# Attention with an MLP mixer on one core: GpSimd's queue in program order, K in quarters, an earlier LN2, and other slots for sums and norm

## The chip, the cores and the metric

The kernel runs on one core of a Trainium2 chip. The metric is the device time of one execution in microseconds (us). The core has five engines that work side by side and wait for each other by semaphores: TensorE (PE, matrix products), VectorE (DVE, elementwise work), ScalarE (ACT, exp, tanh and the like), GpSimd (POOL) and SyncE (SP). DMA transfers are issued from the queues of SP, POOL or ACT.

## What is computed

With x of 2048 tokens by 512 features, K and V caches of 32 heads by 2048 keys by 128, the reference is, cut to what matters:

```
xn = layernorm(x)
q  = (xn @ wq) in 32 heads of 128
p  = softmax(q @ K^T / sqrt(128))          per head, 2048 x 2048
s  = concat(p @ V) @ wo
h  = gelu(layernorm(xn) @ w1)              four quarters of the features,
hs = concat(shifted quarters of h) @ w2    shifted by +1, -1, +2, -2 tokens
x1 = xn + hs
h2 = gelu(layernorm(x1) @ w3) @ w4         w3: 512 x 1792
out = x + s * silu(x1 + h2)
```

Inputs and output are bf16.

## The kernel before

**Units and slots.** The attention is cut into 128 units, each one head and one block of 512 queries (L113). Four heads form a group; a group goes through its four query blocks, and in each through its four heads. A unit has eight slots (SPU = 8, L54). The loop at L507 runs over all slots n; u, p = divmod(n, 8) are the unit and the slot in it. In each slot `s_slot` (L158) issues two score matmuls into one of two score buffers (psS) and the exp on ACT, and `pv_slot` (L187) issues two PV matmuls, five slots behind the scores (LAG = 5, L55). So the first PV of unit u is issued in slot 5 of unit u. Its sum over all keys is built in one PSUM bank, `ps_o`, from a pool of two (L95).

**What else a unit does.** The q projection of the next unit, `q_mm` (L145), in slots 0 and 1, and its copy to bf16, `q_copy` (L153), on DVE in slot 2. DVE adds up the exps of the unit: `add_first` in slot 4, `add_next` in slot 6, and `add_last` (L181) in slot 0 of the next unit, which is a last addition of 2048 columns and two folds (1024 and 512 columns). In slot 3 `sums` (L197) reduces over partitions with four small matmuls (ps_sum), takes the reciprocal on DVE (rc, L204) and sends it to DRAM (dr); in slot 4 `bcast` (L208) reads it back to all partitions (rb). In slot 2 of the unit after that, `norm` (L213) multiplies ps_o by rb into oT, and so frees the ps_o bank: norm(u-2) runs in unit u. After the four heads of a group, the output projection `wo_mm` (L223) of four token tiles takes slots 4 and 5 of the four following units, and `wo_post` (L240) adds it to the float32 sum s_acc in slot 6. The q projection, the sums and the output projection share one PSUM bank (tag xa of psX).

**The MLP** is cut into 136 chunks (L463 to L478), spread evenly over the half units (slots 2 and 3, or 6 and 7; W0 and W1 at L479): 16 of w1 (m1), 16 of the shifted mixer w2 (m2), then for each of four token blocks 14 of w3 (m3) and 12 of w4 (m4). `at(n, fn)` puts follow-up work into later slots: a GELU pair (L281) is a square and a tanh on ACT and two DVE operations, 3 and 7 slots after its matmuls. `ln2` (L378) loads four tiles of x1, normalises them on DVE and transposes them by DMA into xn2T. For the first token block it is called when the mixer's last chunk is done (hook "ph2", L561), together with the opening of the pool that takes the mixer's place (ph2), w4 and three w3 loads; the chunks wait for four half units there.

**Order of the queues.** `pin` (keep_in_program_order, L61) keeps the instructions of an engine in the order of the program. It is used for PE, DVE, ACT and SP work. What GpSimd issues (loads of V, Wq, Wo, the LN tiles, w1 to w4, the stores of xn, x1 and g, and the two operations of `rsqrt`, L108) is not pinned: the framework's scheduler orders it. K comes by transposing DMA on SP in four pieces of 512 keys (`load_k`, L123); in the last query block of a group, head hh of the next group is loaded in unit hh of the block, two pieces in slot 5 and two in slot 7 (L511 to L520).

**The start.** Four x tiles are loaded on SP and ACT and their LN statistics taken, then the loads of head 0, the normalised tiles (xnT by DMA transposes), the loads of heads 1 to 3, the mixer's weights and four Wo tiles. Tiles 4 to 15 are loaded (on GpSimd), measured and normalised in the first slots (L501).

Of the kernel before, what the change touches and what calls it, by code (L numbers as in the profile page):

```python
# [17 lines left out]
def kernel(  # L18
# [71 lines left out]
    gtp = ent(pool("gt", 2))  # L90
    tokp = ent(pool("tok", 3))
    drp = ent(pool("drp", 4, bass.MemoryType.DRAM))
    dsp = ent(pool("dsp", 1, bass.MemoryType.DRAM))
# [14 lines left out]
    def rsqrt(out, var):  # L108
        ve = smp.tile([P, 1], FP32, name="ve")
        nc.gpsimd.tensor_scalar(out=ve[:], in0=var, scalar1=EPS, scalar2=None, op0=ALU.add)  # L110
        nc.gpsimd.tensor_tensor(out=out, in0=ve[:], in1=nhalf[:], op=ALU.pow)

# [19 lines left out]
    def load_v(h):  # L132
        vBs[h] = vp.tile([P, KC, Dh], BF16, name="vb")
        nc.gpsimd.dma_start(  # L134
            out=vBs[h][:], in_=A_v_cache[0, h].rearrange("(kc p) d -> p kc d", p=P))

    def load_w(h):
        wqs[h] = wqp.tile([P, DC, Dh], BF16, name="wq_h")
        nc.gpsimd.dma_start(out=wqs[h][:], in_=wq_v[:, :, h * Dh:(h + 1) * Dh])  # L139

    def load_wo(h):
        wos[h] = wop.tile([P, D], BF16, name="wo_h")
        nc.gpsimd.dma_start(out=wos[h][:], in_=A_wo[h * Dh:(h + 1) * Dh, :])

# [35 lines left out]

    def add_last(u):  # L181
        add_next(u, 3)
        a = st[u]["acc"]
        pin(nc.vector.tensor_tensor(out=a[:, 0:2, :], in0=a[:, 0:2, :], in1=a[:, 2:4, :], op=ALU.add))  # L184
        pin(nc.vector.tensor_tensor(out=a[:, 0, :], in0=a[:, 0, :], in1=a[:, 1, :], op=ALU.add))  # L185
# [47 lines left out]
    def fin_load(t):  # L233
        xl = finp.tile([P, D], BF16, name="xl")
        nc.gpsimd.dma_start(out=xl[:], in_=xsrc[t])
        gl = finp.tile([P, D], BF16, name="gl")
        nc.gpsimd.dma_start(out=gl[:], in_=g_d[t][:])
        fin[t] = (xl, gl)
# [18 lines left out]

    def ln1_stats(t, eng):
        xin = tokp.tile([P, D], BF16, tag="xin", bufs=4, name="xin")
        eng.dma_start(out=xin[:], in_=xsrc[t])  # L260
        bn = smp.tile([P, nc.vector.BN_STATS_DIM], FP32, name="bn")
        mv = smp.tile([P, nc.vector.BN_AGGR_DIM], FP32, name="mv")
        rs = smp.tile([P, 1], FP32, name="rs")
        pin(nc.vector.bn_stats(out=bn[:], in_=xin[:]))
        pin(nc.vector.bn_aggr(out=mv[:], in_=bn[:]))
        rsqrt(rs[:], mv[:, 1:2])
        ln[t] = (xin, mv, rs)

    def ln1_apply(t):
        xin, mv, rs = ln.pop(t)  # L270
        xn = tokp.tile([P, D], BF16, tag="xn", bufs=4, name="xn")
        pin(nc.vector.tensor_scalar(
            out=xn[:], in0=xin[:], scalar1=mv[:, 0:1], scalar2=rs[:],
            op0=ALU.subtract, op1=ALU.mult))
        pin(nc.sync.dma_start_transpose(out=xnT[:, :, t * P:(t + 1) * P], in_=xn[:]))
        nc.gpsimd.dma_start(out=xn_d[t][:], in_=xn[:])

# [49 lines left out]
    def ph1_load():  # L327
        nc.gpsimd.dma_start(out=w1_sb[:], in_=B_w1.rearrange("(dc p) j -> p dc j", p=P))
        nc.gpsimd.dma_start(out=w2_sb[:], in_=B_w2.rearrange("(jc p) c -> p jc c", p=P))
# [14 lines left out]
    def m2_chunk(t):  # L344
        def run(i, n):
            if i == 0:
                mlp["ps"] = psX.tile([P, 512], FP32, tag="xm", name="ps_m")
                mlp["xr"] = tokp.tile([P, D], BF16, tag="xr", bufs=3, name="xr")
                nc.gpsimd.dma_start(out=mlp["xr"][:], in_=xn_d[t][:])
            for jc in (2 * i, 2 * i + 1):  # L350
                c0 = BASE_J[jc] + t * P - SHIFT[jc]
                mm(mlp["ps"][:], hT[:, jc, c0:c0 + P], w2_sb[:, jc, :], jc == 0, jc == DC - 1)
            if i == 1:
                ps, xr = mlp["ps"], mlp["xr"]

                def x1():
                    pin(nc.vector.scalar_tensor_tensor(
                        out=xr[:], in0=ps[:], scalar=0.5, in1=xr[:], op0=ALU.mult, op1=ALU.add))
                    nc.gpsimd.dma_start(out=x1_d[t][:], in_=xr[:])

                def stats():
                    bn = smp.tile([P, nc.vector.BN_STATS_DIM], FP32, name="bn")
                    pin(nc.vector.bn_stats(out=bn[:], in_=xr[:]))
                    pin(nc.vector.bn_aggr(out=mv2[:, t, :], in_=bn[:]))
                    rsqrt(rstd2[:, t:t + 1], mv2[:, t, 1:2])

                at(n + 1, x1)
                at(n + 2, stats)
        return run

    def ph2_open():
# [3 lines left out]
        nc.gpsimd.dma_start(out=w4_sb[:], in_=B_w4.rearrange("(fc p) c -> p fc c", p=P))  # L375
        mlp.update(ph2=ph2, w4=w4_sb, h2={})

    def ln2(c, n):  # L378
        def start():
            mlp["xn2T"] = mlp["ph2"].tile([P, DC, 512], BF16, name="xn2T")  # L380
            xs = []
            for ts in range(4):
                xr = tokp.tile([P, D], BF16, tag="x1", bufs=4, name="x1r")
                nc.gpsimd.dma_start(out=xr[:], in_=x1_d[c * 4 + ts][:])
                xs.append(xr)
            mlp["xs"] = xs
# [33 lines left out]
    def w3_prefetch():  # L420
        if w3_order:
            c, fc = w3_order.popleft()
            w = mlp["ph2"].tile([P, DC, 2 * P], BF16, tag="w3", bufs=3, name="w3_sb")
            nc.gpsimd.dma_start(out=w[:], in_=w3_v[:, :, fc * P:(fc + 2) * P])  # L424
            mlp["w3next"][(c, fc)] = w
# [3 lines left out]
    def m4_chunk(t, part):  # L429
# [3 lines left out]
        def run(i, n):  # L433
            if part == 0 and i == 0:
                mlp["ps"] = psX.tile([P, 512], FP32, tag="xm", name="ps_m")
                mlp["xr"] = tokp.tile([P, D], BF16, tag="xr", bufs=3, name="xr")
                nc.gpsimd.dma_start(out=mlp["xr"][:], in_=x1_d[t][:])
            h = (len(fcs) + 1) // 2
# [3 lines left out]
            if part == 2 and i == 1:  # L442
# [10 lines left out]
                def silu():  # L453
                    pin(nc.vector.scalar_tensor_tensor(
                        out=xr[:], in0=th[:], scalar=1.0, in1=xr[:], op0=ALU.add, op1=ALU.mult))
                    nc.gpsimd.dma_start(out=g_d[t][:], in_=xr[:])

# [6 lines left out]
    for tt in range(QT):  # L464
        for jc in range(DC):
            chunks.append(m1_chunk(tt, jc))
    for t in range(NT):
        chunks.append(m2_chunk(t))
    hooks = {len(chunks): "ph2"}
    for c in range(QT):  # L470
# [12 lines left out]

    ln1_engs = [nc.sync, nc.scalar, nc.sync, nc.scalar]
    for t in range(4):
        ln1_stats(t, ln1_engs[t])
    load_w(0)
    load_k(0, range(KSPLIT))
    load_v(0)
    for t in range(4):  # L490
        ln1_apply(t)
    for h in range(1, HG):
        load_w(h)
        load_k(h, range(KSPLIT))
        load_v(h)
    ph1_load()
    for h in range(HG):
        load_wo(h)
    q_mm(0, range(DC))
    q_copy(0)  # L500
    for k, t in enumerate(range(4, NT)):  # L501
        n0 = 1 + 4 * k
        at(n0, lambda t=t: ln1_stats(t, nc.gpsimd))
        at(n0 + 4, lambda t=t: ln1_apply(t))

    wo_todo = deque()
    for n in range(NS + 3 * SPU):  # L507
        u, p = divmod(n, SPU)
        if u < NU:
            g, qt, hh = units[u]  # L510
            if g + 1 < NG and qt == QT - 1:  # L511
                h = (g + 1) * HG + hh
                if p == 5:
                    load_k(h, (0, 1))
                elif p == 6:
                    load_v(h)
                    load_w(h)
                elif p == 7:
                    load_k(h, (2, 3))
                    load_wo(h)  # L520
            s_slot(u, p)
# [5 lines left out]
        if p == 0 and 1 <= u <= NU:  # L527
            add_last(u - 1)
        if p == 2 and u + 1 < NU:
            q_copy(u + 1)  # L530
        if p == 2 and 2 <= u <= NU + 1:
            norm(u - 2)
            if units[u - 2][2] == HG - 1:
                gg, qq = units[u - 2][:2]
                wo_todo.extend((gg, 4 * qq + ts) for ts in range(4))
                if gg == NG - 1:
                    fin_load(4 * qq)
        if p == 3 and 1 <= u <= NU:
            sums(u - 1)
        if p == 4 and 1 <= u <= NU:  # L540
            bcast(u - 1)
        if p in (4, 5) and wo_todo:
            wo_mm(*wo_todo[0], (0, 1) if p == 4 else (2, 3))
        if p == 6 and wo_todo:
            gg, t = wo_todo.popleft()
            wo_post(gg, t)
            if gg == NG - 1 and t % 4 < 3:
                fin_load(t + 1)
        if p == 4 and u < NU:
            add_first(u)  # L550
# [63 lines left out]
```

## Time and profile before

| what | value |
|---|---|
| median of 3 runs (lowest, highest) | 1346.35 us (1344.34, 1347.98) |
| profiled execution: time, span | 1346.22 us, 1344.4 us |
| granted TensorE clock, mean | 0.985 |
| busy: PE, DVE, ACT, POOL | 95%, 76%, 83%, 16% |
| score matmuls (128x512) | 2048, mean 381 ns as recorded |
| exp on ACT (128x1024) | 1024, mean 1029 ns |
| addition on DVE (128x2048) | 1220 ns |
| norm on DVE (128x512) | 681 ns median |
| rb to landing, K piece to landing | 4.2 us, 4.8 us median |

The span runs from the first to the last instruction on the engines; the time of an execution is a little more. Matmuls are pipelined: one of 512 columns is recorded at 0.38 us, but a pair follows the pair before after 0.43 us. A wait is put down to the instruction whose end released it.

### The profile page before, as it was taken

What the parts mean: (1) busy time and instruction counts of PE and PEld (TensorE: products, weight loads), DVE (VectorE), ACT (ScalarE), POOL (GpSimd) and SP (SyncE); (2) the same over time, 40 slices, a digit from 0 to 9 for tenths busy, and PEclk for the clock granted to TensorE, in tenths of its full rate; (3) what the DMA queues carried; (4) which work ended last, traced back from release to release, by engine and by line L of the source; (5) the groups of instructions that cost most, each with busy time, mean ns of one, the idle gap of its engine ahead of it and who ended that gap; (6) DMA issues with size and microseconds to landing.
All of it is one profiled execution on the core that took longest, in us unless ns stands there. A gap on an engine that the chain in (4) does not pass through costs nothing.

```text
span 1344.4 us, 17137 instructions
## 1 busy us (share of the span) xinstructions
PE 1275.2 (95%) x6208; PEld 576.4 (43%) x6208; DVE 1024.1 (76%) x1402; ACT 1112.8 (83%) x1185; POOL 212.4 (16%) x343
## 2 busy tenths in 40 slices
PE   2899999999599999999999999999999999999996
PEld 1344444444244444444444444444444444444442
DVE  1898788887377886778877767888767788777886
ACT  2799988787399987889998888999878999888882
POOL 6620122323101012010111001110010100000111
PEclk9999999999799999999999999999999999999997
DMA  9830383326722239222473215522273222812223
GB/s 213 182 87 25 71 135 71 76 59 144 154 56 59 45 67 158 63 52 46 91 131 75 52 36 124 100 61 42 56 137 68 64 47 48 125 34 52 81 66 90
DMA packets 144260, 112.29 MB, mean 84 GB/s; under 512 B 112112, under 2 KB 114672, under 8 KB 144176
## 3 DMA queue, kind: packets, MB, share of 16 engines
q1 hardware_dynamic: 126496, 57.19, 24.3%
q0 software_dynamic: 17392, 53.76, 15.9%
q8 instruction: 48, 0.79, 0.3%
q14 instruction: 36, 0.29, 0.1%
q10 hardware_dynamic: 288, 0.26, 0.1%
HBM read 81.53 MB, written 8.65 MB: 67 GB/s over the span
## 4 chain that ended last, share of the span: by engine, by line
PE 74%; DVE 9%; DMA 8%; ACT 5%; issue 3%; POOL 1%; SPq 0%; DVEq 0%; POOLq 0%
PE ps_s L106 27%; PE ps_o L106 25%; PE ps_wo L106 8%; PE ps_m L106 8%; PE ps_q L106 6%; ACT pT L168 4%; DMA rb<-dr 3%; DVE acc L179 3%; DMA dr<-rc 2%; PE ps_sum L106 1%; DVE acc L184 1%; DVE qT L155 1%; DMA xin<-in_A_x_dram 1%; ACT sq L286 1%; DMA xn2T<-x1r 1%
## 5 line engine op out<-in xcount | busy, mean ns | idle before, releaser
L168 ACT ACTIVATE pT<-ps_s 128x1024 bf16<-128x1024 f32 x1024 | 1015.7, 1029 | 205.0 <-PE ps_s L106 200.4
L106 PE MATMUL ps_s<-qT,kT 128*128 128x512 bf16 x2048 | 612.1, 381 | 5.5 <-DVE qT L155 2.4
L106 PE MATMUL ps_o<-pT,vb 128*128 128x512 bf16 x2048 | 610.7, 380 | 0.0
L179 DVE TENSOR_TENSOR acc<-acc,pT 128x2048 bf16<-128x2048 bf16 x256 | 312.4, 1220 | 84.9 <-ACT pT L168 80.1
L106 PEld LDWEIGHTS <-vb 128*128 128x128 bf16 x2048 | 200.2, 98 | 243.6 <-issue 3.0
L106 PEld LDWEIGHTS <-kT 128*128 128x128 bf16 x2048 | 196.7, 98 | 245.3 <-issue 28.3
L174 DVE TENSOR_TENSOR acc<-pT 128x2048 bf16<-128x2048 bf16 x128 | 155.8, 1217 | 29.1 <-ACT pT L168 29.0
L106 PE MATMUL ps_q<-xnT,wq_h 128*128 128x512 bf16 x512 | 153.9, 383 | 20.7 <-DMA xnT<-xn 20.7
L106 PE MATMUL ps_wo<-wo_h,oT 128*128 128x512 bf16 x512 | 156.6, 390 | 15.2 <-DVE rc L204 9.7
L246 DVE TENSOR_TENSOR s_acc<-ps_wo,s_acc 128x512 f32<-128x512 f32 x112 | 77.3, 690 | 99.3 <-PE ps_wo L106 99.3
L218 DVE TENSOR_TENSOR oT<-ps_o,rb 128x512 bf16<-128x512 f32 x128 | 87.2, 682 | 18.6 <-DMA rb<-dr 18.4
L155 DVE CAST qT<-ps_q 128x512 bf16<-128x512 f32 x128 | 87.3, 682 | 13.6 <-PE ps_q L106 13.6
L184 DVE TENSOR_TENSOR acc<-acc 128x1024 bf16<-128x1024 bf16 x128 | 88.6, 692 | 4.4
L106 PEld LDWEIGHTS <-oT 128*128 128x128 bf16 x512 | 50.7, 99 | 82.9 <-issue 24.9
L106 PEld LDWEIGHTS <-wq_h 128*128 128x128 bf16 x512 | 50.4, 99 | 82.1 <-DMA wq_h<-in_A_wq_dram 20.6
L106 PE MATMUL ps_m<-xn2T,w_sb 128*128 128x512 bf16 x224 | 67.4, 383 | 11.1 <-DMA xn2T<-x1r 11.1
L106 PE MATMUL ps_m<-w_sb,h2T 128*128 128x512 bf16 x224 | 63.9, 379 | 0.0
L424 POOL DMA_DIRECT2D w_sb<-in_B_w_dram x28 | 21.2, 756 | 264.3 <-PE ps_m L106 249.4
L185 DVE TENSOR_TENSOR acc<-acc 128x512 bf16<-128x512 bf16 x128 | 54.4, 425 | 4.4
L139 POOL DMA_DIRECT2D wq_h<-in_A_wq_dram x32 | 24.5, 765 | 206.3 <-PE ps_q L106 192.4
L106 PEld LDWEIGHTS <-acc 128*128 128x128 bf16 x512 | 37.3, 116 | 44.7 <-issue 13.5
L134 POOL DMA_DIRECT2D vb<-in_A_v_cache_dram x32 | 37.4, 1167 | 111.2 <-PE ps_o L106 107.5
(51 smaller groups left out, 599.4 us busy)
## 6 DMA issues: line engine op xcount, KB each, us to landing
rb<-dr SPq DMA_DIRECT2D x128, 256.0 KB, 4.2
vb<-in_A_v_cache_dram POOLq DMA_DIRECT2D x32, 512.0 KB, 7.5
w_sb<-in_B_w_dram POOLq DMA_DIRECT2D x28, 256.0 KB, 4.4
wq_h<-in_A_wq_dram POOLq DMA_DIRECT2D x32, 128.0 KB, 3.2
wo_h<-in_A_wo_dram POOLq DMA_DIRECT2D x32, 128.0 KB, 4.6
kT<-in_A_k_cache_dram SPq DMA_TRANSPOSE x128, 4.8
xn_d<-xn POOLq DMA_DIRECT2D x16, 128.0 KB, 3.3
xr<-xn_d POOLq DMA_DIRECT2D x16, 128.0 KB, 3.9
```

The lines of the kernel that those rows point to most:

```text
L106: pin(nc.tensor.matmul(out=out, lhsT=lhsT, rhs=rhs, start=start, stop=stop))
L134: nc.gpsimd.dma_start(out=vBs[h][:], in_=A_v_cache[0, h].rearrange("(kc p) d -> p kc d", p=P))
L139: nc.gpsimd.dma_start(out=wqs[h][:], in_=wq_v[:, :, h * Dh:(h + 1) * Dh])
L155: pin(nc.vector.tensor_copy(out=qT[:], in_=st[u].pop("psq")[:]))
L168: pin(nc.scalar.activation(out=s["pT"][-1][:, jj:jj + 2, :], in_=sps[:], func=ACT.Exp, scale=SCALE))
L174: pin(nc.vector.tensor_tensor(out=s["acc"][:], in0=s["pT"][0][:], in1=s["pT"][1][:], op=ALU.add))
L179: pin(nc.vector.tensor_tensor(out=a[:], in0=a[:], in1=st[u]["pT"][i][:], op=ALU.add))
L184: pin(nc.vector.tensor_tensor(out=a[:, 0:2, :], in0=a[:, 0:2, :], in1=a[:, 2:4, :], op=ALU.add))
L185: pin(nc.vector.tensor_tensor(out=a[:, 0, :], in0=a[:, 0, :], in1=a[:, 1, :], op=ALU.add))
L218: pin(nc.vector.tensor_tensor(out=oTs[(g, qt)][:, hh, :], in0=s["o"][:], in1=s["rb"][:], op=ALU.mult))
L246: pin(nc.vector.tensor_tensor(out=sa, in0=ps[:], in1=sa, op=ALU.add))
L424: nc.gpsimd.dma_start(out=w[:], in_=w3_v[:, :, fc * P:(fc + 2) * P])
```

## The change

All that GpSimd issues is now pinned to program order, through a helper `load`. The functions of the diff do this:

- The x tiles of the start are loaded by `ln1_load`: 0 to 3 on SP and ACT, 4 to 7 on ACT after tile t - 4 has been normalised, 8 and on in slots 4k - 8 on GpSimd. The mixer's weights come in slot 3, the four Wo tiles in slots 12 to 24.
- `refill` takes the place of the loads in slots 5 to 7: half units are counted from the beginning of the next group, and each K piece, V, Wq and Wo tile has its own half unit, issued in slot 1 or 6.
- `add_last` is split: the last addition stays in slot 0, the two folds go to slot 2 behind the q copy. `sums` goes from slot 3 to 4, `norm` from slot 2 to 4 behind it, `bcast` from 4 to 5, `wo_mm` from 4 and 5 to 5 and 6, `wo_post` from 6 to 7. `add_first` and `add_next` stay in slots 4 and 6.
- xn2T and the w3 tiles get pools of their own (xn2p; w3p with three buffers). LN2 of the first token block and two w3 loads are hooked before the ninth m2 chunk; at the hook "ph2" only the pool is opened and w4 loaded, and the chunks wait for one half unit.

The core of the diff (where only `nc.gpsimd.dma_start` becomes `load`, it is left out):

```diff
+    xn2p = ent(pool("xn2p"))
+    w3p = ent(pool("w3p", 3))
...
-        nc.gpsimd.tensor_scalar(out=ve[:], in0=var, scalar1=EPS, scalar2=None, op0=ALU.add)
-        nc.gpsimd.tensor_tensor(out=out, in0=ve[:], in1=nhalf[:], op=ALU.pow)
+        pin(nc.gpsimd.tensor_scalar(out=ve[:], in0=var, scalar1=EPS, scalar2=None, op0=ALU.add))
+        pin(nc.gpsimd.tensor_tensor(out=out, in0=ve[:], in1=nhalf[:], op=ALU.pow))
+
+    def load(out, in_, eng=None):
+        pin((eng or nc.gpsimd).dma_start(out=out, in_=in_))
...
-    def add_last(u):
-        add_next(u, 3)
+    def folds(u):
         a = st[u]["acc"]
...
-    def ln1_stats(t, eng):
-        xin = tokp.tile([P, D], BF16, tag="xin", bufs=4, name="xin")
-        eng.dma_start(out=xin[:], in_=xsrc[t])
+    def ln1_load(t, eng=None):
+        ln[t] = tokp.tile([P, D], BF16, tag="xin", bufs=4, name="xin")
+        load(out=ln[t][:], in_=xsrc[t], eng=eng)
+
+    def ln1_stats(t):
+        xin = ln[t]
...
-            mlp["xn2T"] = mlp["ph2"].tile([P, DC, 512], BF16, name="xn2T")
+            mlp["xn2T"] = xn2p.tile([P, DC, 512], BF16, name="xn2T")
...
-            w = mlp["ph2"].tile([P, DC, 2 * P], BF16, tag="w3", bufs=3, name="w3_sb")
-            nc.gpsimd.dma_start(out=w[:], in_=w3_v[:, :, fc * P:(fc + 2) * P])
+            w = w3p.tile([P, DC, 2 * P], BF16, name="w3_sb")
+            load(out=w[:], in_=w3_v[:, :, fc * P:(fc + 2) * P])
...
+    hooks = {}
     for t in range(NT):
+        if t == 8:
+            hooks[len(chunks)] = 0
         chunks.append(m2_chunk(t))
-    hooks = {len(chunks): "ph2"}
+    hooks[len(chunks)] = "ph2"
...
-    ln1_engs = [nc.sync, nc.scalar, nc.sync, nc.scalar]
     for t in range(4):
-        ln1_stats(t, ln1_engs[t])
+        ln1_load(t, (nc.sync, nc.scalar)[t % 2])
     load_w(0)
     load_k(0, range(KSPLIT))
     load_v(0)
     for t in range(4):
+        ln1_stats(t)
+    for t in range(4):
         ln1_apply(t)
+        ln1_load(t + 4, nc.scalar)
     for h in range(1, HG):
         load_w(h)
         load_k(h, range(KSPLIT))
         load_v(h)
-    ph1_load()
-    for h in range(HG):
-        load_wo(h)
     q_mm(0, range(DC))
     q_copy(0)
+    at(3, ph1_load)
+    for h in range(HG):
+        at(12 + 4 * h, lambda h=h: load_wo(h))
     for k, t in enumerate(range(4, NT)):
-        n0 = 1 + 4 * k
-        at(n0, lambda t=t: ln1_stats(t, nc.gpsimd))
-        at(n0 + 4, lambda t=t: ln1_apply(t))
+        if k >= 4:
+            at(4 * k - 8, lambda t=t: ln1_load(t))
+        at(4 * k + 1, lambda t=t: ln1_stats(t))
+        at(4 * k + 3, lambda t=t: ln1_apply(t))
+
+    WQ_AT, WO_AT, V_AT = (-4, 0, 3, 5), (-2, 1, 5, 8), (-3, 4, 7, 9)
+
+    def refill(gn, hu):
+        if not 1 <= gn < NG:
+            return
+        for hh in range(HG):
+            h = gn * HG + hh
+            if hh == 0:
+                if hu in (-6, -4, -2, 0):
+                    load_k(h, ((hu + 6) // 2,))
+            elif 0 <= hu - (4 * hh - 2) < KSPLIT:
+                load_k(h, (hu - (4 * hh - 2),))
+            if hu == V_AT[hh]:
+                load_v(h)
+            if hu == WQ_AT[hh]:
+                load_w(h)
+            if hu == WO_AT[hh]:
+                load_wo(h)
 
     wo_todo = deque()
     for n in range(NS + 3 * SPU):
         u, p = divmod(n, SPU)
         if u < NU:
             g, qt, hh = units[u]
-            if g + 1 < NG and qt == QT - 1:
-                h = (g + 1) * HG + hh
-                if p == 5:
-                    load_k(h, (0, 1))
-                elif p == 6:
-                    load_v(h)
-                    load_w(h)
-                elif p == 7:
-                    load_k(h, (2, 3))
-                    load_wo(h)
+            if p in (1, 6):
+                hu = 2 * (qt * HG + hh) + (p == 6)
+                refill(g + 1, hu - 24)
+                refill(g, hu + 8)
             s_slot(u, p)
         m = n - LAG
         if 0 <= m < NS:
@@ -525,31 +551,34 @@
         if p in (0, 1) and u + 1 < NU:
             q_mm(u + 1, (2 * p, 2 * p + 1))
         if p == 0 and 1 <= u <= NU:
-            add_last(u - 1)
-        if p == 2 and u + 1 < NU:
-            q_copy(u + 1)
-        if p == 2 and 2 <= u <= NU + 1:
+            add_next(u - 1, 3)
+        if p == 2:
+            if u + 1 < NU:
+                q_copy(u + 1)
+            if 1 <= u <= NU:
+                folds(u - 1)
+        if p == 4 and 1 <= u <= NU:
+            sums(u - 1)
+        if p == 4 and 2 <= u <= NU + 1:
             norm(u - 2)
             if units[u - 2][2] == HG - 1:
                 gg, qq = units[u - 2][:2]
                 wo_todo.extend((gg, 4 * qq + ts) for ts in range(4))
                 if gg == NG - 1:
                     fin_load(4 * qq)
-        if p == 3 and 1 <= u <= NU:
-            sums(u - 1)
-        if p == 4 and 1 <= u <= NU:
+        if p == 5 and 1 <= u <= NU:
             bcast(u - 1)
-        if p in (4, 5) and wo_todo:
-            wo_mm(*wo_todo[0], (0, 1) if p == 4 else (2, 3))
-        if p == 6 and wo_todo:
+        if p in (5, 6) and wo_todo:
+            wo_mm(*wo_todo[0], (0, 1) if p == 5 else (2, 3))
+        if p == 4 and u < NU:
+            add_first(u)
+        if p == 6 and u < NU:
+            add_next(u, 2)
+        if p == 7 and wo_todo:
             gg, t = wo_todo.popleft()
             wo_post(gg, t)
             if gg == NG - 1 and t % 4 < 3:
                 fin_load(t + 1)
-        if p == 4 and u < NU:
-            add_first(u)
-        if p == 6 and u < NU:
-            add_next(u, 2)
         if p in (2, 3, 6, 7):
             w = 2 * u + (p >= 4)
             i = p % 2
@@ -560,13 +589,13 @@
                     hook = hooks.pop(done, None)
                     if hook == "ph2":
                         ph2_open()
-                        for _ in range(3):
-                            w3_prefetch()
-                        ln2(0, n)
-                        W0 += 4
-                        W1 += 4
+                        W0 += 1
+                        W1 += 1
                     else:
                         if hook is not None:
+                            if hook == 0:
+                                w3_prefetch()
+                                w3_prefetch()
                             ln2(hook, n)
                         window["run"] = chunks.popleft()
                         done += 1
```

More of the change, by code (lines that the diff above doesn't have):

```diff
@@ L133, in load_v @@
         vBs[h] = vp.tile([P, KC, Dh], BF16, name="vb")
-        nc.gpsimd.dma_start(
+        load(
             out=vBs[h][:], in_=A_v_cache[0, h].rearrange("(kc p) d -> p kc d", p=P))
@@ L138, in load_w @@
         wqs[h] = wqp.tile([P, DC, Dh], BF16, name="wq_h")
-        nc.gpsimd.dma_start(out=wqs[h][:], in_=wq_v[:, :, h * Dh:(h + 1) * Dh])
+        load(out=wqs[h][:], in_=wq_v[:, :, h * Dh:(h + 1) * Dh])
     def load_wo(h):
         wos[h] = wop.tile([P, D], BF16, name="wo_h")
-        nc.gpsimd.dma_start(out=wos[h][:], in_=A_wo[h * Dh:(h + 1) * Dh, :])
+        load(out=wos[h][:], in_=A_wo[h * Dh:(h + 1) * Dh, :])
     def q_mm(u, dcs):
@@ L234, in fin_load @@
         xl = finp.tile([P, D], BF16, name="xl")
-        nc.gpsimd.dma_start(out=xl[:], in_=xsrc[t])
+        load(out=xl[:], in_=xsrc[t])
         gl = finp.tile([P, D], BF16, name="gl")
-        nc.gpsimd.dma_start(out=gl[:], in_=g_d[t][:])
+        load(out=gl[:], in_=g_d[t][:])
         fin[t] = (xl, gl)
@@ L275, in ln1_apply @@
         pin(nc.sync.dma_start_transpose(out=xnT[:, :, t * P:(t + 1) * P], in_=xn[:]))
-        nc.gpsimd.dma_start(out=xn_d[t][:], in_=xn[:])
+        load(out=xn_d[t][:], in_=xn[:])
     mlp = {}
@@ L327, in ph1_load @@
     def ph1_load():
-        nc.gpsimd.dma_start(out=w1_sb[:], in_=B_w1.rearrange("(dc p) j -> p dc j", p=P))
-        nc.gpsimd.dma_start(out=w2_sb[:], in_=B_w2.rearrange("(jc p) c -> p jc c", p=P))
+        load(out=w1_sb[:], in_=B_w1.rearrange("(dc p) j -> p dc j", p=P))
+        load(out=w2_sb[:], in_=B_w2.rearrange("(jc p) c -> p jc c", p=P))
         for jc in range(DC):
@@ L348, in run @@
                 mlp["xr"] = tokp.tile([P, D], BF16, tag="xr", bufs=3, name="xr")
-                nc.gpsimd.dma_start(out=mlp["xr"][:], in_=xn_d[t][:])
+                load(out=mlp["xr"][:], in_=xn_d[t][:])
             for jc in (2 * i, 2 * i + 1):
@@ L358, in x1 @@
                         out=xr[:], in0=ps[:], scalar=0.5, in1=xr[:], op0=ALU.mult, op1=ALU.add))
-                    nc.gpsimd.dma_start(out=x1_d[t][:], in_=xr[:])
+                    load(out=x1_d[t][:], in_=xr[:])
                 def stats():
@@ L374, in ph2_open @@
         w4_sb = ph2.tile([P, FC, D], BF16, name="w4_sb")
-        nc.gpsimd.dma_start(out=w4_sb[:], in_=B_w4.rearrange("(fc p) c -> p fc c", p=P))
+        load(out=w4_sb[:], in_=B_w4.rearrange("(fc p) c -> p fc c", p=P))
         mlp.update(ph2=ph2, w4=w4_sb, h2={})
@@ L383, in start @@
                 xr = tokp.tile([P, D], BF16, tag="x1", bufs=4, name="x1r")
-                nc.gpsimd.dma_start(out=xr[:], in_=x1_d[c * 4 + ts][:])
+                load(out=xr[:], in_=x1_d[c * 4 + ts][:])
                 xs.append(xr)
@@ L436, in run @@
                 mlp["xr"] = tokp.tile([P, D], BF16, tag="xr", bufs=3, name="xr")
-                nc.gpsimd.dma_start(out=mlp["xr"][:], in_=x1_d[t][:])
+                load(out=mlp["xr"][:], in_=x1_d[t][:])
             h = (len(fcs) + 1) // 2
@@ L455, in silu @@
                         out=xr[:], in0=th[:], scalar=1.0, in1=xr[:], op0=ALU.add, op1=ALU.mult))
-                    nc.gpsimd.dma_start(out=g_d[t][:], in_=xr[:])
+                    load(out=g_d[t][:], in_=xr[:])
                 at(n + 1, x2)
```

## The prediction

> **What bounds the kernel now.** I read the page's busy shares first, then the busy time of TensorE (PE) by stage, then the list of what PE waited for, and at last the order of single instructions inside one unit (one head times 512 queries: eight slots, each two score matmuls and two PV matmuls, 128 units in all).
>
> ```profile
> span 1344.4 us, 17137 instructions
> ...
> PE 1275.2 (95%) x6208; PEld 576.4 (43%) x6208; DVE 1024.1 (76%) x1402; ACT 1112.8 (83%) x1185; POOL 212.4 (16%) x343
> ```
>
> PE is busy for 95% of the span, so only 1344.4 - 1275.2 = 69.2 us can be won by taking waits away. The next answer says where they lie (columns: stretch, its length, PE busy with its matmuls, granted clock, DMA share, GB/s).
>
> ```profile
> 0.00:20.60 20.60, 0.00 (x0) 1.00 0.98 188
> 20.60:60.00 39.40, 31.45 (x127) 0.96 1.00 227
> 60.00:300.00 240.00, 234.71 (x1155) 1.00 0.35 75
> 300.00:372.00 72.00, 55.05 (x251) 0.88 0.64 141
> 372.00:1318.00 946.00, 939.90 (x4637) 1.00 0.37 73
> 1318.00:1344.40 26.40, 14.04 (x44) 0.62 0.34 89
> ```
>
> Length less busy time gives the idle: 20.6 us before the first matmul, 7.9 until 60, 5.3 until 300, 17.0 in the stretch from 300 to 372, where the mixer passes over to the second half of the MLP, only 6.1 in the 946 us after it, and 12.4 in the tail. In the long stretch PE is busy 99.4% of the time. There every wait that a change gives PE is added to the span whole; nothing else is late beside it.
>
> ```profile
> PE ps_q L106 <- DMA xnT<-xn: 20.7, 1, 20.7
> PE ps_m L106 <- DMA xn2T<-x1r: 11.1, 1, 11.1
> PE ps_wo L106 <- DVE rc L204: 9.7, 8, 4.0
> PE ps_sum L106 <- DVE qT L155: 9.0, 13, 3.6
> ```
>
> These are the waits (us in total, times, longest) that the change speaks of: the start, the missing transposed LN2 input at the hand-over, and reciprocals or q copies that VectorE (DVE) brings late. No wait for a PV bank (ps_o) is in the list. Last, five instructions of a steady unit, in order of time (start, us, engine, line):
>
> ```profile
> 950.81 0.68 DVE L218 TENSOR_TENSOR oT<-ps_o,rb 128x512 bf16<-128x512 f32 x1
> ...
> 951.73 0.27 PE L106 MATMUL ps_sum<-ones_t,acc 128*128 128x1 bf16 x4
> ...
> 951.86 0.59 PE L106 MATMUL ps_s<-qT,kT 128*128 128x512 bf16 x2
> ...
> 952.03 0.18 DVE L204 RECIPROCAL rc<-ps_sum 128x4 f32<-128x4 f32 x1 [0.22 <-PE ps_sum L106]
> ...
> 952.29 0.59 PE L106 MATMUL ps_o<-pT,vb 128*128 128x512 bf16 x2
> ```
>
> From the start of the four sums, PE comes to its next score pair after 0.13 us and to the PV pair behind that after 0.56 us; DVE's reciprocal starts 0.30 us after the sums. The norm (oT, which reads ps_o) is 0.9 us ahead of the sums here.
>
> **The part that costs: norm in slot 4.** The diff puts sums, reciprocal and then norm(u-2) into slot 4. PV runs five slots behind the scores, so the PV of unit u begins in slot 5 of unit u. There are two PV banks: unit u takes the one that norm(u-2) frees. Before, the norm stood in slot 2, three slots ahead of that need; now it stands in the slot just before it, and on DVE's in-order queue it stands behind a reciprocal that waits for PE's own sums of the same slot. PE's way from the sums to PV(u,0) is one score pair, 0.56 us after the sums' start. DVE's way is: 0.30 to the reciprocal, 0.09 from its start to the next operation (324.23 to 324.32 in the trace), 0.68 for the norm, 0.06 from DVE's end to PE's start (23.27 to 23.33, qT to ps_s): 1.13 us. PE waits 0.57 us in each unit from 2 to 127: 126 x 0.57 = **72 us**. What is queued behind it on PE is everything: the PV pair, the wo pair, the next scores. DVE's idle time can't hide it, since the chain starts at PE.
>
> Two smaller costs come with it. (a) A GELU operation of 1.22 us that is due in slot 2 (36 pairs, one each) now lies between the folds and the reciprocal. By the slot times it ends 0.3 us after the sums' result where that half unit has no MLP matmuls of its own, which is about half of them: 18 x 0.3 = 5 us. (b) wo_post moves from slot 6 to 7 and behind add_next. The bank that it frees is the one that the q matmuls of the next slot 0 take. add_first from the norm's end (1.24), add_next (1.24), a GELU operation in slot 6 (1.22) and wo_post (0.69) end some 0.5 us after PE comes there, again in about 18 units: 9 us. Both lean on slot arithmetic: bounds 0 and 16 us, I take 12, since in each a row of 1.22 us has to fit into less slack than that. Without such an operation, wo_post ends 0.7 us ahead of the need and costs nothing.
>
> **The parts that win.** LN2's first tile begins eight mixer chunks early (136 chunks in 236 half units: 8 x 236/136 x 4 = 55 slots ahead), with its own pools, where its work needs 14 slots and a transpose of 3.3 us. The 11.1 us wait goes. In the same stretch K bursts held up the reciprocals' broadcast (DVE's norm waited 4.11 us for rb at 346.8, and PE 4.0 for rc); K in quarters, one per half unit, takes that away too. Idle in the stretch 17.0 us, and time at a low clock: 3.3 us around 350 and 5.3 us from 363.5, where a pair takes 0.85 us instead of 0.43, so half of 8.6, 4.3 us. Together 21.3 us; I take **21**. What is late next there is nothing but the new norm wait, which is counted above. The idle of the other steady stretches, 5.3 + 6.1 us, is mostly the same late norm, q copy and reciprocal: bounds 0 and 11.4, I take **9**, as the broadcast gets one slot more and K no longer comes in fours.
>
> The start: the pinned queue puts each pow behind its add (before, all four pows started only at 8.08, behind a load of 0.76), so the first xn can come when the statistics end at 7.0 instead of 8.7. But DMA is at 98% share until 20.6, and the transposes of xn still stand behind four K transposes on SyncE's queue: bounds 0 and 3, I take 1. Inputs 4 to 7 are loaded from the start on ScalarE's queue, whose exps begin only at 24.4, so DVE doesn't stand 9.9 us for xin at 33.2 with a q copy behind it: PE's waits of 2.4 and 3.6 us go, and 1.8 us of half clock behind the second one. Against it stands the first broadcast, still behind twelve K transposes that SyncE issues until 40.2, and now needed by slot 21 or 47 us: its rows here land at 51.3. I take 6 - 1 = 5 net for the whole, bounds -3 and 11: **6** with the first matmul.
>
> Pinning itself and the moved V, Wq and Wo loads I cost at nothing: a POOL issue takes 0.55 to 1.17 us, POOL is busy 16%, and each load stands more than a unit (10 us) ahead of its use, against 3.2 to 7.5 us to landing. SyncE gets no instruction more, the same 128 K pieces. Without that cover, a late V would cost up to its 7.5 us once per head, 28 x 7.5 = 210 us at the far end; nothing in the new places comes near it. The tail's chain (rc, dr, rb, norm, wo, out) is the same: 0, give or take 1.
>
> **Sum.** 72 + 12 - 21 - 9 - 6 = +48 us on the span of 1344.4: 1392. The profiled execution took 1346.22, 1.8 us around its span, and the median of the runs is 1346.35, so the same offset serves: **1394 us**.
>
> **A rule on the clock.** Row first:
>
> ```profile
> 325.00:335.00 10.00, 8.68 (x44) 1.00 0.85 249
> ...
> 344.00:352.00 8.00, 4.05 (x11) 0.79 0.67 147
> ```
>
> A stop of 1.3 us left the granted clock at 1.00; 4.0 us brought it down. So 0.57 us should leave it, and the sum has no term for the clock. The Trainium skill, TensorE: Matmul & The Clock Gate, section "A second HAM failure mode: psum-queue depth-cycling", speaks against that: a PE that pauses briefly but often as it cycles PSUM banks may swing between half and full clock. By it the sum would be that of the last rival below, near 1594. I follow the row.
>
> **Rivals.** *Faster: the bank is free in time.* If PE's wait for the norm stays under (21 + 9 + 6 - 12)/126 = 0.19 us per unit, the wins prevail; with none, and without the small costs, the time is 1346 - 36 = 1310. For it: PE shows no ps_o wait now, and DVE idles 24%. Against it: the reciprocal is queued ahead of the norm and can't start before PE's sums, so DVE can't run ahead. 13%. *The stall, but no wins:* LN2 begins early on paper, but its loads stick in the pinned POOL queue, or K quarters disturb rb as before: 1346 + 72 + 12 = 1430 at most; 4%. *Near balance*, a stall of about 0.2 us: 1340 to 1355; 4%. *The clock falls* after each short stall as it did after the one of 4.0 us, where 3.3 us at half clock lost 1.6: 126 x 1.6 = 200 us on top of the forecast, 1594; 2%. The forecast within its bounds (a stall of 0.5 to 0.65 us gives 63 to 82, small costs 0 to 16, wins 18 to 44), 1365 to 1426 with all ends together: 77%.
>
> The range 1362 to 1430 leaves out the faster rival, most of the balance and the falling clock, about 2 in 10. A measurement here tells a difference from about 0.3%, 4 us; the balance case splits one, two, one: faster 0.14, same 0.02, slower 0.84.
>
> **What would show it.** Right: in PE's waits a new entry ps_o <- DVE oT, some 126 times, 70 us or more, with a mean of 0.57; PE's busy share in the long stretch down from 99% to 94%; no xn2T wait and no clock dip near 350; K issues one by one. The prediction is wrong if ps_o shows no wait, if DVE runs the norm ahead of the reciprocal, or if the clock of the steady stretch falls below 1.00.

## The result and the profile after

The changed kernel takes 1397.43 us (median; 1396.13 to 1397.91), the kernel before 1346.64 us (1344.34 to 1347.98). The ratio is 1.0377, with a 95% interval of 1.0359 to 1.0395: slower by 51 us. The forecast was 1394. The profiled execution took 1397.68 us, with a span of 1395.9. These are the page's busy shares and the stretches of PE, as for the kernel before (stretch, length, PE busy with its matmuls, granted clock, DMA share, GB/s):

```profile
PE 1285.9 (92%) x6208; PEld 574.7 (41%) x6208; DVE 1011.6 (72%) x1402; ACT 1112.2 (80%) x1185; POOL 217.8 (16%) x339
```

```profile
0.00:20.70 20.70, 0.00 (x0) 1.00 1.03 210
20.70:60.00 39.30, 35.32 (x157) 1.00 0.82 181
60.00:300.00 240.00, 224.08 (x1079) 0.99 0.38 76
300.00:372.00 72.00, 64.56 (x316) 1.00 0.54 131
372.00:1345.00 973.00, 927.28 (x4511) 1.00 0.35 71
```

The start and the hand-over at 300 to 372 are better than before: 157 matmuls by 60 us where there were 127, and 7.4 us of idle where there were 17.0, at a clock of 1.00. (The 0.99 between 60 and 300 is one short fall of the clock, from 207 to 211 us; more of it below.) But the long stretch, 99.4% busy before, is now 95.3% busy: 45.7 us idle. PE's waits say why (total, times, longest):

```profile
PE ps_o L108 <- DVE oT L222: 51.1, 119, 1.6
PE ps_q L108 <- DMA wq_h<-in_A_wq_dram: 20.8, 1, 20.8
PE ps_q L108 <- DVE s_acc L250: 9.9, 17, 0.6
PE ps_sum L108 <- DVE acc L189: 6.2, 5, 2.3
PE ps_wo L108 <- DVE oT L222: 3.8, 1, 3.8
PE ps_q L108 <- DVE s_acc L248: 3.7, 7, 0.8
```

The waits for xn2T are gone, and those for late q copies but for one of 0.8 us. A new one stands on top: the first PV pair of a unit waits for the norm that frees its bank, 119 times. One such place in order of time (start, us, engine, line):

```profile
709.51 0.27 PE L108 MATMUL ps_sum<-ones_t,acc 128*128 128x1 bf16 x4
...
709.64 0.59 PE L108 MATMUL ps_s<-qT,kT 128*128 128x512 bf16 x2
709.82 0.18 DVE L208 RECIPROCAL rc<-ps_sum 128x4 f32<-128x4 f32 x1 [1.81 <-PE ps_sum L108]
...
709.92 0.66 DVE L222 TENSOR_TENSOR oT<-ps_o,rb 128x512 bf16<-128x512 f32 x1
...
710.63 0.59 PE L108 MATMUL ps_o<-pT,vb 128*128 128x512 bf16 x2 [0.40 <-DVE oT L222]
```

From the sums to the PV pair it is 1.12 us; before it was 0.56. So PE loses 0.56 us here, though the bracket says 0.40: the record lets the pair before end 0.16 us after the moment at which a next pair would have started (a pair is recorded with 0.59 us, and pairs follow each other in 0.43). This 0.16 has to be added to each recorded wait of PE that follows a pair. VectorE had been idle for 1.81 us ahead of the reciprocal: it could have done the norm long before, had the reciprocal not been ahead of it.

### The profile page after: what moved, and what is told of

Its sections match the earlier page's. It is cut to its first block, busy times and chain, and to the rows that moved or that the text cites. A ratio compares the mean times of both kernels' runs of the same rounds, so it can differ in the third digit from the quotient of the medians.

```text
span 1395.9 us, 17081 instructions
## 1 busy us (share of the span) xinstructions
PE 1285.9 (92%) x6208; PEld 574.7 (41%) x6208; DVE 1011.6 (72%) x1402; ACT 1112.2 (80%) x1185; POOL 217.8 (16%) x339
## 4 chain that ended last, share of the span: by engine, by line
PE 65%; DVE 13%; ACT 12%; DMA 5%; issue 3%; POOL 1%; DVEq 0%; POOLq 0%; ACTq 0%; SPq 0%
PE ps_o L108 23%; PE ps_s L108 21%; ACT pT L173 8%; PE ps_m L108 7%; PE ps_q L108 7%; PE ps_wo L108 6%; DVE oT L222 4%; DVE acc L184 3%; ACT sq L293 2%; DMA rb<-dr 2%; ACT pre L323 1%; DVE rc L208 1%; DVE acc L179 1%; DVE s_acc L250 1%; DMA xr<-xn_d 1%
## 5 line engine op out<-in xcount | busy, mean ns | idle before, releaser
L108 PE MATMUL ps_o<-pT,vb 128*128 128x512 bf16 x2048 | 608.5, 379 | 51.1 <-DVE oT L222 51.1
L108 PEld LDWEIGHTS <-kT 128*128 128x128 bf16 x2048 | 192.2, 98 | 224.6 <-issue 23.4
L108 PE MATMUL ps_q<-xnT,wq_h 128*128 128x512 bf16 x512 | 153.7, 382 | 34.4 <-DMA wq_h<-in_A_wq_dram 20.8
L208 DVE RECIPROCAL rc<-ps_sum 128x4 f32<-128x4 f32 x128 | 23.4, 182 | 141.8 <-PE ps_sum L108 140.3
L108 PEld LDWEIGHTS <-wq_h 128*128 128x128 bf16 x512 | 50.3, 98 | 99.4 <-issue 22.0
L116 POOL DMA_DIRECT2D g_d<-xr x16 | 8.8, 550 | 437.1 <-DVE xr L461 413.1
```

The costliest lines, as they stand in the source:

```text
L108: pin(nc.tensor.matmul(out=out, lhsT=lhsT, rhs=rhs, start=start, stop=stop))
L116: pin((eng or nc.gpsimd).dma_start(out=out, in_=in_))
L208: pin(nc.vector.reciprocal(out=rc[:], in_=ps[:]))
```

## The experiments

Each was compared with the kernel before on its own chip, whose median was 1344 to 1350 us, so ratios are compared where two runs come from different chips. Several expectations name times from the chip on which the kernel before took 1344 us and the old slots 1322; on a chip whose kernel before takes 1350 they lie some 5 us higher.

**The slots of before in the changed kernel.** The edit puts the calls back:

```diff
         if p == 0 and 1 <= u <= NU:
             add_next(u - 1, 3)
+            folds(u - 1)
...
-        if p == 4 and 1 <= u <= NU:
+        if p == 3 and 1 <= u <= NU:
             sums(u - 1)
-        if p == 4 and 2 <= u <= NU + 1:
+        if p == 2 and 2 <= u <= NU + 1:
             norm(u - 2)
```

and likewise bcast (slot 4), wo_mm (4, 5) and wo_post (6, ahead of add_next).

> The changed kernel with the slots of before (folds in 0, norm in 2, sums in 3, bcast in 4, wo_mm in 4 and 5, wo_post in 6); pinned queue, K quarters, early LN2 and start stay. My theory (the slots cost, the rest wins): 1397 less 71 for the norm wait and 17 for the wait for the q bank, about 1310, range 1303 to 1320, and no ps_o wait. Rival (the pinned GpSimd queue or the K quarters make the loss): above 1346, with the stalls still in the trace.

Measured: 1322.3 us (1321.38 to 1323.93), ratio 0.9835 (0.9809 to 0.9861). The ps_o wait is gone, so the slot moves cost 73 us by the ratios (75 by the times) and all the rest wins 22 to 24. That is 2 us above the range that I gave: the wins are smaller than forecast. PE's waits in this run show one reason, old waits that the slot moves had taken away:

```profile
PE ps_sum L108 <- DVE qT L160: 9.4, 16, 1.9
PE ps_wo L108 <- DVE rc L208: 4.9, 6, 1.2
```

**Norm ahead of the reciprocal, nothing else.** PE's order of instructions is unchanged:

```diff
-        if p == 4 and 1 <= u <= NU:
-            sums(u - 1)
         if p == 4 and 2 <= u <= NU + 1:
             norm(u - 2)
...
+        if p == 4 and 1 <= u <= NU:
+            sums(u - 1)
```

> The changed kernel with two calls swapped in slot 4: norm(u-2) is issued to VectorE ahead of the sums and their reciprocal. PE's order is the same. My theory (the norm is late because it is queued behind a reciprocal that waits for PE's own sums): the ps_o wait goes, 1397 less 71, about 1326, range 1318 to 1336; the waits for s_acc stay. Rival (slot 4 itself is too late for a bank needed in slot 5, whatever the order): still at least 0.2 us of ps_o wait per unit, 1350 or more.

Measured: 1349.39 us (1347.56 to 1350.92), ratio 1.0035 (1.0007 to 1.0063). The swap of two calls brings back 46 us by the ratios (48 by the times), so the place behind the reciprocal is shown to be the main cause. But it is not the 71 that I expected, and neither theory's number was met:

```profile
PE ps_q L108 <- DVE s_acc L250: 16.9, 21, 1.1
PE ps_o L108 <- DVE oT L222: 8.1, 23, 1.5
PE ps_q L108 <- DVE s_acc L248: 5.6, 9, 1.1
```

The waits for s_acc have grown from 13.6 us in 24 to 22.5 in 30, since PE now comes to the q bank 0.56 us earlier; and in 23 units the norm is still late. With 0.16 for each: 10 us and 12 us, and 70 - 10 - 12 = 48. One wait had hidden part of another. Of the 23 late norms, 16 stand directly behind a GELU operation of VectorE, and three wait for a late broadcast.

**The slot moves alone in the kernel before.** The block of slots of the changed kernel in the old loop, no other part of the change.

> The kernel before with only the slot moves. My theory: 1346 plus 71 for the norm and about 10 to 17 for the q bank, less 0 to 9 of old waits for rc and qT that the moves remove: 1418 to 1434. Rival (the slot moves are harmless, another part costs): within 10 of 1346.

Measured: 1415.34 us (1413.32 to 1417.81), ratio 1.0527 (1.0497 to 1.0556), 71 us more than before. The theory's direction and size hold; it lies 3 us under the range. Two things that my sum did not have pull against each other. The moves take away more old waits than the 9 us that I allowed: what PE waited for rc and, ahead of its sums, for the q copy falls from 18.7 us in 21 to 0.3 in 1. And at the hand-over one norm waited 13.6 us for a broadcast that took 13.0 us to land, so that PE waited 14.1 us for the bank, and then less for xn2T (4.0 instead of 11.1):

```profile
PE ps_o L106 <- DVE oT L217: 63.9, 120, 14.1
...
PE ps_m L106 <- DMA xn2T<-x1r: 4.0, 1, 4.0
```

**A larger dose.** add_first is put between the reciprocal and the norm:

```diff
             sums(u - 1)
+        if p == 4 and u < NU:
+            add_first(u)
         if p == 4 and 2 <= u <= NU + 1:
             norm(u - 2)
```

> The changed kernel with add_first (1.22 us on VectorE) put between the reciprocal and the norm. My theory (PE pays VectorE's chain in full): 1.24 us more in each of 126 units, 156 us, less up to 17 as the q bank is then free in time: 1536 to 1553, clock still 0.99. Rival (longer pauses of 1.8 us, 126 times, pull the granted clock down): above 1600, clock below 0.95. Rival (PE's time is partly bound elsewhere, so that a wait is only partly paid): under 1500.

Measured: 1514.55 us (1513.55 to 1515.55), clock 0.993; 117 us more than the changed kernel (119 by the ratios), under the range. In order of time:

```profile
703.00 0.27 PE L108 MATMUL ps_sum<-ones_t,acc 128*128 128x1 bf16 x4
...
703.31 0.18 DVE L208 RECIPROCAL rc<-ps_sum 128x4 f32<-128x4 f32 x1
...
703.41 1.19 DVE L179 TENSOR_TENSOR acc<-pT 128x2048 bf16<-128x2048 bf16 x1
...
704.52 0.68 DVE L222 TENSOR_TENSOR oT<-ps_o,rb 128x512 bf16<-128x512 f32 x1
...
705.26 0.59 PE L108 MATMUL ps_o<-pT,vb 128*128 128x512 bf16 x2 [1.53 <-DVE oT L222]
```

The chain is 2.26 us instead of 1.12, so 1.14 us more and not 1.24 (the norm starts 1.11 us after add_first). 126 x 1.14 = 144; the recorded ps_o waits say the same, 193.2 us in 126 against 51.1 in 119. From this go 17 us of s_acc waits, of which none is left, and 5 for waits for the folds: 122, against 117 measured. So PE pays VectorE's chain in full, up to the 5 us between the two, and the longer pauses don't touch the clock: it is 1.00 from 60 to 1490 us.

**Norm in slot 3, wo_post in slot 6.** An attempt at new slots without either wait:

```diff
-        if p == 4 and 2 <= u <= NU + 1:
+        if p == 3 and 2 <= u <= NU + 1:
             norm(u - 2)
...
-        if p == 7 and wo_todo:
+        if p == 6 and wo_todo:
             gg, t = wo_todo.popleft()
```

with norm ahead of the sums, and wo_post ahead of add_next.

> The changed kernel with norm in slot 3 (so ahead of the sums of slot 4 and two slots ahead of the bank's need) and wo_post in slot 6 ahead of add_next. My theory (two waits of the slot moves make all of the loss: the norm behind the reciprocal, and wo_post behind add_next, with 0.16 us to add to each recorded wait): both entries go from PE's list, so 1397 less about 75, 1318 to 1326, like the run with the old slots (1322). Rival (the moved folds and sums carry a cost of their own): 1335 or more, with waits for acc or rc in their place.

Measured: 1332.89 us (1330.23 to 1336.0), ratio 0.988 (0.9858 to 0.9903): better than the kernel before, but by the ratios some 6 us behind the old slots (0.9835), give or take 5. It lies between the theory's range and the rival's. The s_acc wait ahead of ps_q is gone; the norm wait is not.

```profile
PE ps_o L108 <- DVE oT L222: 11.7, 24, 3.1
PE ps_s L108 <- ACT pT L173: 5.7, 22, 0.4
PE ps_sum L108 <- DVE acc L189: 5.6, 6, 2.6
```

```profile
DVE oT L222 <- DMA rb<-dr: 17.5, 12, 4.6
```

The norm itself now waits for the broadcast, 17.5 us in 12 units, and it stands only two slots ahead of the need. In the old slots there are three, and there the norm's waits for the broadcast, 15.3 us in 12, give PE no ps_o wait. Six of these late broadcasts reach PE and make 7 of the 11.7 us; in most of the other places a GELU operation stands directly ahead of the norm, nearly always with a wait of 0.16 to 0.18 us. PE's waits for the folded sums (acc) are 5.6 us in 6 against 2.5 in 2 with the old slots, so the rival is right for some 4 us, with the 0.16.

**Only wo_post back in slot 6.**

> The changed kernel with only wo_post put back into slot 6, ahead of add_next. My theory (the second cost is the q bank, 24 recorded waits of together 13.6 us and 0.16 us more on each, 17 us): no s_acc wait ahead of ps_q, the norm wait unchanged at 0.56 us per unit, about 1380, range 1375 to 1386. Rival (that wait only hides what the norm wait would take up): 1390 or more.

Measured: 1390.61 us (1389.12 to 1392.08), ratio 1.031 (1.0283 to 1.0338). Against the changed kernel's ratio that is 0.0067, 9 us, and not 17.

```profile
PE ps_o L108 <- DVE oT L222: 52.3, 119, 2.3
...
PE ps_s L108 <- ACT pT L173: 7.8, 22, 0.7
```

No s_acc wait ahead of ps_q is left, and the norm wait stays, as the theory has it. But the scores now wait for ACT 22 times instead of 9, 7.8 us instead of 3.0; with 0.16 for each, 7 of the 17 us come back there. The rival's number is nearly met, but not for its reason: the scores took up the hidden part, not the norm.

**The queue left to the scheduler again** (old slots; GpSimd's DMAs and the two operations of rsqrt unpinned):

> The run with the old slots (1322), and GpSimd's own instructions left to the scheduler's order again. Theory (pinning by itself is worth nothing either way): within 5 of 1322. Rival (the pinned queue issues the mixer's xr loads so late that VectorE waits for them, and that ate the win I had expected in the steady stretches): 1310 to 1316. Rival (pinning is what made the early loads and the start good): 1328 or more.

Measured: 1323.85 us (1322.24 to 1328.64), ratio 0.9819 (0.9796 to 0.9842), against 0.9835. The intervals overlap: with all else of the change in place, pinning is worth nothing that can be seen.

**LN2 late again** (old slots):

```diff
-        if t == 8:
-            hooks[len(chunks)] = 0
...
                         ph2_open()
-                        W0 += 1
-                        W1 += 1
+                        for _ in range(3):
+                            w3_prefetch()
+                        ln2(0, n)
+                        W0 += 4
+                        W1 += 4
```

> The run with the old slots (1322), with LN2 of the first block and its three w3 loads called at the mixer's end again and four half units of pause; xn2T and w3 keep their own pools. My theory (the early start of LN2 is worth the xn2T wait and its clock dip): 1334 to 1342, an xn2T wait of about 11 us. Rival (the own pools are what counts, since the old ones had to wait for the mixer's pool): below 1327, with an xn2T wait under 3 us.

Measured: 1338.76 us (1336.79 to 1346.1), ratio 0.9925 (0.99 to 0.995). Against 0.9835 the early LN2 is worth about 12 us, give or take 5 by the intervals (15 by the spans, 1335.0 and 1320.4, from two chips). The total is as expected, so the rival, that the own pools are all that counts, falls. The wait is not:

```profile
PE ps_wo L108 <- DVE rc L208: 10.8, 7, 3.4
PE ps_sum L108 <- DVE qT L160: 7.9, 14, 1.5
PE ps_m L108 <- DMA xn2T<-x1r: 4.0, 1, 4.0
```

xn2T costs 4.0 us and not 11. The last of its four transposes landed 4.7 us after its issue here, and 8.4 us in the kernel before. What held it up there, the old pools, the K bursts or something else, was not tested: the run with the slot moves alone has old pools and bursts and a wait of 4.0 us, but PE had just stood 14.1 us for a norm.

**K in bursts again** (old slots; two pieces in slot 5 and two in slot 7 of the last query block):

> The run with the old slots (1322), with K's next heads loaded in two bursts of two pieces per unit in the last query block, as before. My prediction's term (late broadcasts in the steady stretches come from the bursts, 9 us): 1328 to 1334. Rival (the old slots' run has as many rb waits with quarters as the kernel before had with bursts, so quarters bring nothing): 1319 to 1325.

Measured: 1329.32 us (1323.63 to 1333.53), ratio 0.9845 (0.982 to 0.987), against 0.9835 with quarters: 1 us apart, and the intervals leave room for 6 at most. The 1329 us lie in the range of my term as it was put, but that range was reckoned from 1344 us for the kernel before, which takes 1350 on this chip; by the ratios the term of 9 us for the quarters falls. VectorE waited 24.5 us for rb here and 16.2 in the repeat of the old slots below, but little of that reaches PE.

**The old start, with the queue pinned** (old slots). xin is loaded in the slot of its statistics and normalised four slots later; the mixer's weights and Wo are loaded ahead of the first matmul again:

```diff
-        if k >= 4:
-            at(4 * k - 8, lambda t=t: ln1_load(t))
-        at(4 * k + 1, lambda t=t: ln1_stats(t))
-        at(4 * k + 3, lambda t=t: ln1_apply(t))
+        at(4 * k + 1, lambda t=t: (ln1_load(t), ln1_stats(t)))
+        at(4 * k + 5, lambda t=t: ln1_apply(t))
```

> The run with the old slots (1322), with the start of before: x tiles 4 on are loaded on GpSimd in the slot of their statistics and normalised four slots later, the mixer's weights and Wo are loaded ahead of the first matmul; GpSimd stays pinned. My prediction's term (6 us, from the waits for xin and the half clock after 42 us, none from the first matmul): 4 to 9 above the run with the old slots of this call. Rival (the start is bound by DMA either way): within 2.

> The run with the old slots once more, as the reference on this chip for the run with the old start: ratio 0.981 to 0.986 to the kernel before.

Measured: the old start 1379.46 us (1378.5 to 1387.29), ratio 1.0239 (1.0209 to 1.0268); the old slots again 1327.06 us (1322.34 to 1331.99), ratio 0.9835 (0.9806 to 0.9864). The old start is 52 us slower, which no theory of mine held possible. GpSimd's queue in order of time:

```profile
36.61 0.62 POOL L116 DMA_DIRECT2D xn_d<-xn  x1 [1.36 <-DVE xn L279]
37.23 0.54 POOL L116 DMA_DIRECT2D xin<-in_A_x_dram  x1
41.41 1.09 POOL L112 TENSOR_SCALAR ve<-mv 128x1 f32<-128x1 f32 x1 [3.63 <-DVE mv L272]
42.59 1.60 POOL L113 TENSOR_TENSOR rs<-ve,nhalf 128x1 f32<-128x1 f32 x1
45.56 0.64 POOL L116 DMA_DIRECT2D xn_d<-xn  x1 [1.37 <-DVE xn L279]
46.20 0.54 POOL L116 DMA_DIRECT2D xin<-in_A_x_dram  x1
```

Each load of xin stands behind the store of the tile before, and that store waits for VectorE. VectorE's next operation in order needs that very load. So a full transfer (issued at 37.23, statistics at 40.40) is exposed for each of 12 tiles, with the q copy behind it.

**Pinning alone, in the kernel before.**

> The kernel before with GpSimd's queue pinned to program order and nothing else changed. Theory after the run with the old start (each xin load is queued behind a store of xn that waits for VectorE, and VectorE then waits for the load): some 55 us of VectorE waits for xin and 45 to 60 us more than before, 1390 to 1410, all of it before 150 us of the span or at the mixer's end. Rival (pinning is neutral by itself, and the old start was slow for another part of that run): within 8 of the kernel before.

Measured: 1418.69 us (1418.03 to 1420.57), ratio 1.0528 (1.0499 to 1.0557): 70 us more than before, 9 above the range. Waits of VectorE and of PE:

```profile
DVE bn L267 <- DMA xin<-in_A_x_dram: 63.1, 13, 11.9
...
DVE x1r L394 <- DMA x1r<-x_d: 9.6, 1, 9.6
```

```profile
PE ps_sum L106 <- DVE qT L158: 54.3, 17, 9.2
```

The 63.1 us for xin are there as expected, and at the beginning of unit 7 the run is 46 us behind the kernel before. At unit 32, after the mixer's end, it is 58: there VectorE waits 9.6 us for x1r, which the range had not counted. This is not the same pattern: directly ahead of the four x1r loads stand the loads of V, Wq, w4 and w3, and no store; they were issued from 386.1 to 394.1 us and took up to 16.8 us to land. The remaining 14 us come later, and I have no cause for them. So the rival falls: pinning by itself costs as much as the slot moves do. The earlier loads of xin make the larger part of it harmless; which part of the change takes the wait for x1r away is open, since the pinned run with the late LN2 has none either.

## Why the prediction was right

**The norm wait, 72 us: right in mechanism and size.** 1.12 us from the sums to the PV pair against 1.13 forecast; 119 recorded waits of 51.1 us, with 0.16 on each, are 70. The sign that I had named, some 126 entries of together 70 us, is in the list only with this 0.16. The clock term of zero was right too: 1.00 in the long stretch, and still 1.00 there in the run with add_first, whose 126 pauses were 1.7 us. The one fall of the clock before the tail, 3.4 us at half clock behind a recorded wait of 1.4 us for the folds and one of 0.4 us for the norm, cost 1.7 us. What the Trainium skill reports of another kernel, TensorE: Matmul & The Clock Gate, section "A second HAM failure mode: psum-queue depth-cycling", that frequent short pauses made the clock swing, does not show in the long stretch of this kernel.

**The two small costs, 12 us: under-sized, and one missed.** (b), the q bank behind wo_post, is 13.6 us recorded in 24 waits, 17 with the 0.16, where I had 9. In 18 of the 24 places a GELU operation stands ahead of wo_post, as I had counted, but each costs 0.80 us and not 0.5; the other six stand behind the mixer's residual and its statistics, which I had not counted. (a), GELU operations ahead of the reciprocal, lengthened only two norm waits, by together 0.9 us, where I had 5. The norm waits above the usual 0.40 come to 51.1 - 119 x 0.40 = 3.5 us, and most of that is three late broadcasts. What I had not at all is the wait of PE's sums for the folds, which now come in slot 2: 6.2 us in 5 against 2.5 in 2 with the old slots, 4 us with the 0.16. Three of the five follow a wait of VectorE for a load of the mixer's xr, 5.9 us in all.

**The steady stretches, -9 us: about the right size, but not by the quarters.** I gave it to a broadcast with one slot more and to the K quarters; the quarters are worth nothing that can be measured. PE's waits for qT and rc between 60 and 300 and from 372 to 1318, 9.3 us in 17 in the kernel before, are gone in the changed kernel, but not with the old slots (10.3 in 18). So the slot moves take them away. Over the whole of the old slots' run these waits are 14.3 us in 22, 18 with the 0.16, and the slot moves come to 70 + 17 + 4 - 18 = 73 us, which is what undoing them gave by the ratios.

**The hand-over, -21 us: 3 us too large.** I gave the whole stretch to the early LN2 and the K quarters together. From the first exp of unit 30 to that of unit 36 the kernel before takes 78.5 us and the run with the old slots 60.1, so 18 us are won there. The early start of LN2 is 12 to 15 of the total; in this stretch the run with the late LN2 takes 70.8. How the rest divides between the quarters, the own pools and the shorter pause of the chunks was not tested.

**The start, -6 us: right in size.** Thirty matmuls more by 60 us, at 0.2 us each, are 6. Nothing came from the first matmul, which starts at 20.8 us instead of 20.7.

**Pinning, 0: right only beside the other parts.** My step said that POOL is idle enough and that each load stands a unit ahead of its use. That holds for the changed kernel. I never asked what the pin would do to the old places, where a load stands behind a store that waits for VectorE. It costs 70 us alone, 46 of them in the first seven units, where those places are.

The sum came out at +48 against +51, with some luck: the new costs were taken 7 us too small (91 against 84) and the removed old waits 9 us too small, which nearly cancels, while the hand-over was taken 3 us too large and the tail is 2 us longer. The best version run here is the change without its slot moves: 0.9835 (0.9806 to 0.9864), 22 us faster than before, with the queue pinned or not.

## What to carry to other kernels

Before moving an operation that frees a buffer, count the slots until the buffer is needed again, and look at what stands ahead of it in its engine's queue: if that waits for the engine that needs the buffer, no idle time of its own engine helps. Pinning a queue that a scheduler used to order freely turns every place where a load follows a store into a possible round trip, so move the loads forward with it. And when two waits lie close together, taking one away gives back less than its own length, since the other grows.

## What the runs showed of the hardware

The norm took 659 ns (median) in the changed kernel, directly behind the reciprocal, and 681 ns in the kernel before. With add_first between the two it took 684 ns, though PE was waiting there as well, so it is not PE's pause that makes it shorter; what does was not tested. Pauses of 1.7 us in every unit, some 11.5 us apart, left the granted clock at 1.00, while the stretch from 20.7 to 60 us of the run with the old start, with one pause of 10.9 us in it, had 0.83. The length of a single pause did not decide it between 1 and 3 us: waits of 2.4 us (kernel before, until 34.8 us) and 2.3 us (changed kernel, until 338.5) left the clock at 1.00, but in the changed kernel waits of 1.4 and 0.4 us close together were followed by 3.4 us at half clock (mean 0.57 from 207 to 211), and in the repeat of the old slots single waits of 2.0 and 2.1 us were too (0.66 from 320 to 325, 0.57 from 812 to 816). What else decides was not tested.
